# Maxima over partitions by TensorE and VectorE, and an order of work found in 40 passes, in a kernel of pooled attention and two MoE layers

## Chip, cores and metric

The kernel runs on one core of a Trainium2 chip. The metric is the time of one execution on the device in microseconds (us); less is better. The profile is that of one execution, taken by the hardware profiler.

## What is computed

Attention over 4 batches and 8 heads of 64, whose 1152 queries are averaged in pairs to 576, and then two feed-forward layers on the 2304 resulting rows of 512:

```python
q_pool = q.reshape(B, H, S // 2, 2, D).mean(axis=3)
scores = np.matmul(q_pool, k.transpose(0, 1, 3, 2)) / np.sqrt(D)
attn = np.exp(scores - np.max(scores, axis=-1, keepdims=True))
attn = attn / (np.sum(attn, axis=-1, keepdims=True) + 1e-09)
x = np.matmul(attn, v)                # then (B * 576, H * D)
h = x @ w_in                          # 512 -> 2048
x = (h / (1.0 + np.exp(-h))) @ w_out  # 2048 -> 512
a, b = x @ w1, x @ w2                 # 512 -> 1024 each
out = (a * b @ w3) @ w_out2           # 1024 -> 1024 -> 512
```

The weights come as float64; the outputs are float32.

## The kernel before

Matrix products with float32 operands take several passes on TensorE, so the kernel splits most operands into two float16 halves (`hi` and `lo`, scaled by a power of two) and adds three products (`TERMS`). The scale needs the largest absolute value of the tensor. VectorE reduces along the free dimension to one value per partition, and `allmax` (line 309) reduces over the 128 partitions on GpSimd, for the 12 stagings of V (line 431), the 9 blocks of attention output (line 653), the two first weights (line 768), w1 and w2 together (line 887) and the 6 inputs of the last stage: 30 in all. `pow2` (line 301) makes the power of two from it.

Attention goes by batch, half of the queries (`g`), pair of heads (`hp`), and tile of 128 queries, 144 tiles in all. `tile_ops` (line 446) issues one tile: scores into PSUM (`qk`, L465), the row maxima (L502, VectorE), the exponentials with their sum (L482, ScalarE), the inverse of the sum (L487, L490). In batches 1 to 3 the probabilities are split into halves (L530, L493) and transposed by a DMA (L498). In batch 0 (`b < WHOLE`) there are no halves: TensorE transposes the float32 tile (L514), ScalarE copies it out (L517), and the inverse of the sum is laid out by a VectorE tile `dg` (L523) and a small float32 matmul (`spread`, L562). Scores and transposes share two PSUM tiles of three banks (`t_s`). `pv_ops` (line 585) multiplies by V (L610, or L555 in batch 0) into one of two one-bank PSUM tiles (`t_mm`) and evacuates to `x32`, a float32 buffer for a block of 256 rows by 512; there is one such buffer, and one for the 64-row tails of the four batches.

`block_ops` (line 626) takes a block through the first MoE: the maximum of `x32` (L632), the all-reduce, the scales, the halves `x16` (L656, L643), eight `h_unit` steps (L676, two times twelve matmuls each), the gate on ScalarE and VectorE, its halves (L698 on ScalarE, L701 on GpSimd), and sixteen `x_unit` steps (L717). There are nine blocks, two per batch and one of the tails. `weights_moe1` (line 738) turns w_in and w_out, 16 chunks of 128 x 512 each, from float64 to float32 by integer operations (`from_f64`, L328 to L330), takes their maxima (L760) and splits them (L783, L788). After attention its buffers are given to the second MoE: w1, w2 and w_out2 are turned and split, w3 is multiplied by w_out2 beforehand (L1015), and six blocks of 384 rows run through L1119 and L1163.

The order of work on each engine is not the program's. Every step is an `op` with an engine, an estimated cost, a due time (`key`) and the buffers that it reads and writes; `Plan.run` (line 115) is a list scheduler that simulates the engines with these costs. At each turn it takes, of the steps that an engine could start within 0.15 us, the one with the smallest key:

```python
go = max(free[e], min(at for at, _ in can))
at, o = min(((at, o) for at, o in can if at <= go + 0.15), key=lambda x: (x[1].key, x[1].n))
```

The keys are written by hand, in units of attention tiles (for instance `i - 1.5` for the scores of tile `i`, `key - 12` for the halves of the gate). The instructions are then issued in the order that this one pass gives, and each engine works through its own list strictly in that order. All loads, stores and DMA transposes are issued from the queue of SP.

Of the kernel before, what the change touches and what calls it, by code (L numbers as in the profile page):

```python
# [9 lines left out]
F32 = mybir.dt.float32  # L10
# [17 lines left out]
LOAD_AFTER = 3.0  # L28
AFTER = {PE: 0.25, ACT: 0.2, DVE: 0.15, POOL: 0.2, SP: 0.0}
# [28 lines left out]
class Op:  # L58
    __slots__ = (
        "eng", "cost", "land", "fn", "key", "after", "need", "ready", "start", "end", "takes", "bufs", "n", "hook",  # L60
        "placed",
# [3 lines left out]
class Plan:  # L65
# [5 lines left out]
    def op(self, eng, cost, fn, r=(), w=(), key=0.0, land=None):  # L71
# [3 lines left out]
        o.n, o.hook = len(self.ops), None  # L75
# [39 lines left out]
    def run(self):  # L115
        cand = defaultdict(list)
        free = {e: 0.0 for e in ENGINES}
        free["CTL"] = 0.0
        order = []
# [17 lines left out]
        while any(cand.values()):  # L137
# [11 lines left out]
            assert best is not None, [o.n for some in cand.values() for o in some][:20]  # L149
            at, e, o = best  # L150
            cand[e].remove(o)
            o.start = at
            if e != "CTL":
                free[e] = at + o.cost
            o.end = at + (o.cost if o.land is None else o.land)
# [3 lines left out]
            for buf in o.takes:  # L159
                tag = buf.tag  # L160
                buf.place = min(tag.free, key=lambda s: (tag.free[s], s))
                del tag.free[buf.place]
                tag.next += 1
            for buf in o.bufs:
                buf.left -= 1
                buf.end = max(buf.end, o.end + AFTER.get(e, 0.0))
                if buf.left == 0:
                    buf.tag.free[buf.place] = buf.end
            for x in o.after:
# [15 lines left out]
def kernel(  # L185
# [51 lines left out]
    ident_b = Buf(Tag(1))  # L237

# [27 lines left out]
    t_dg = tags(attn, "dg", 4, [P, D])  # L266
# [42 lines left out]
    def allmax(dst, src):  # L309
        nc.gpsimd.partition_all_reduce(dst, src, channels=P, reduce_op=bass_isa.ReduceOp.max)  # L310

    def from_f64(dst, words, dst_b, words_b, key):
# [20 lines left out]
        op(DVE, 1.85, merge, [words_b], [dst_b], key + 0.01)  # L333
# [13 lines left out]

    kts, qts, v16s, mvs = {}, {}, {}, {}
# [14 lines left out]
    def prep_q(b, g, hp):  # L363
# [20 lines left out]
        op(DVE, 0.7 + 0.13 * g, pool, [qs], [qt], i0 - 7)  # L384

    def prep_v(b, hp):
        i0 = FIRST_T[(b, 0, hp)]
        v16, mv = attn_buf(t_v16), attn_buf(t_mv) if b >= WHOLE else None
# [10 lines left out]

        def top():  # L400
            nc.vector.reduce_max(mv.t[:, 0:1], vs.t, axis=AX.X, apply_absolute_value=True)

        def scales():
            pow2(mv.t[:, 1:2], mv.t[:, 2:3], mv.t[:, 3:4])
            nc.vector.tensor_scalar_mul(mv.t[:, 3:4], mv.t[:, 3:4], 2.0 ** 13)
            nc.vector.tensor_scalar_mul(mv.t[:, 4:5], mv.t[:, 2:3], 2.0 ** -29)

        def hi():
            d_, s_ = parts()
            nc.scalar.activation(d_[:, :, 0, :], s_, AF.Copy, scale=mv.t[:, 3:4])  # L410

        def lo():
            d_, s_ = parts()
            nc.vector.scalar_tensor_tensor(
                d_[:, :, 1, :], s_, mv.t[:, 3:4], d_[:, :, 0, :], op0=ALU.mult, op1=ALU.subtract
            )
# [13 lines left out]
        op(DVE, 1.36, top, [vs], [(mv, 0)], i0 - 4)  # L430
        op(POOL, 0.4, lambda: allmax(mv.t[:, 1:2], mv.t[:, 0:1]), [(mv, 0)], [(mv, 1)], i0 - 3.9)
        op(DVE, 0.8, scales, [(mv, 1)], [(mv, 2)], i0 - 2)
        op(ACT, 1.26, hi, [vs, (mv, 2)], [(v16, 0)], i0 - 1)
        op(DVE, 1.45, lo, [vs, (mv, 2), (v16, 0)], [(v16, 1)], i0 + 0.5)

    WHOLE = 1
    pts = {}
    x32s = {}  # L440
    dgs = {}

# [3 lines left out]
    def tile_ops(i):  # L446
# [53 lines left out]
        op(PE, 1.14, qk, [kt, qt], [sc], i - 1.5)  # L500
# [4 lines left out]
        op(ACT, 1.43, soft_exp, [sc, (sm, 0)], [e, (sm, 1)], i - 3.0 * whole)  # L505
        op(DVE, 0.32, inverse, [(sm, 1)], [(sm, 2)], i + 0.2)
        if whole:
            st, dg = Buf(t_s), attn_buf(t_dg)
            dgs[i] = dg
# [9 lines left out]
            op(PE, 1.1, turn32, [e, ident_b], [st, (pt, (j % 2, 0))], i + 0.3)  # L519
# [13 lines left out]
        op(DVE, 1.45, lo, [e, (sm, 2), (p16, 0)], [(p16, 1)], i + 0.8)  # L533
        op(SP, 2.75, turn, [p16], [(pt, j % 2)], i + 1, land=5.2)

    def pv_whole(b, g, hp, i, last, ps, nn, mine, x32, off):
# [22 lines left out]
        def spread():  # L559
            for (a, jj), dg in inv.items():  # L560
# [3 lines left out]
                    dg.t,  # L564
# [6 lines left out]
        op(  # L571
            PE, 0.3 if last else 0.6, spread, [ident_b] + [dg for k_, dg in inv.items() if not last or k_ == (0, 0)],
# [3 lines left out]
        op(PE, 1.4 if last else 4.5, pv, [v16] + list(mine.values()), [ps, (x32, (hp, off, 0))], i + 2.5)  # L576
# [8 lines left out]
    def pv_ops(b, g, hp, i, last=False):  # L585

        v16, mv = v16s[(b, hp)], mvs[(b, hp)]
# [4 lines left out]
        if blk not in x32s:  # L592
            x32s[blk] = attn_buf(t_x32t if last else t_x32)
        x32 = x32s[blk]
# [23 lines left out]

        def evac():
            nc.scalar.activation(x32.t[:, hp, off : off + nn], ps.t[:, :nn], AF.Copy, scale=mv.t[:, 4:5])  # L620

        op(PE, 1.2 if last else 2.95, pv, [v16] + list(mine.values()), [ps, (x32, (hp, off, 0))], i + 2.5)
        op(ACT, 0.3 if last else 0.45, evac, [ps, (mv, 2)], [(x32, (hp, off))], i - SOON)


    def block_ops(blk, i, span):

        x32, xm = x32s[blk], moe_buf(t_xm)
        x16 = moe_buf(t_x16)
# [612 lines left out]
```

## Time and profile before

| | |
|---|---|
| median of 3 runs | 1200.62 us (1199.74 to 1205.22) |
| the profiled execution | 1200.74 us |
| its span, first to last instruction | 1198.7 us |
[...]
| TensorE (PE) busy | 1108.2 us, 92% |
| VectorE (DVE) busy | 792.2 us, 66% |
| ScalarE (ACT) busy | 663.2 us, 55% |
| GpSimd (POOL) busy | 158.1 us, 13% |

The shares are means over stages that differ: batch 0's attention with the weights of the first MoE (to about 250 us), attention of batches 1 to 3 beside the first MoE (to 755 us), the last blocks of the first MoE beside the weights of the second (to 860 us), and the second MoE. PE is TensorE's matmuls, PEld its weight loads, which run beside them. An idle time is put down to what ended it; "issue" means that nothing that the profile shows ended it.

### The profile page before, as it was taken

What the parts mean: (1) busy time and instruction counts of PE and PEld (TensorE: products, weight loads), DVE (VectorE), ACT (ScalarE), POOL (GpSimd) and SP (SyncE); (2) the same over time, 40 slices, a digit from 0 to 9 for tenths busy, and PEclk for the clock granted to TensorE, in tenths of its full rate; (3) what the DMA queues carried; (4) which work ended last, traced back from release to release, by engine and by line L of the source; (5) the groups of instructions that cost most, each with busy time, mean ns of one, the idle gap of its engine ahead of it and who ended that gap; (6) DMA issues with size and microseconds to landing.
All of it is one profiled execution on the core that took longest, in us unless ns stands there. A gap on an engine that the chain in (4) does not pass through costs nothing.

```text
span 1198.7 us, 21922 instructions
## 1 busy us (share of the span) xinstructions
PE 1108.2 (92%) x8972; PEld 809.1 (67%) x8972; DVE 792.2 (66%) x1283; ACT 663.2 (55%) x986; POOL 158.1 (13%) x156
## 2 busy tenths in 40 slices
PE   3778897999999999999899999897999999999998
PEld 2445675767776767677677777786756776767666
DVE  6988898498788788797987785576977521212110
ACT  3656667567677577686686675465634322222221
POOL 0000120012012012020020020112121111111211
PEclk9978998999999999999999999898999999999999
DMA  9635344368988997989979778454334001010001
GB/s 348 211 134 184 115 140 157 115 136 169 181 182 171 218 194 166 190 174 200 199 145 200 151 123 148 147 194 137 124 123 150 1 27 54 12 42 27 10 18 27
DMA packets 294821, 163.17 MB, mean 136 GB/s; under 512 B 256064, under 2 KB 266816, under 8 KB 294720
## 3 DMA queue, kind: packets, MB, share of 16 engines
q1 hardware_dynamic: 294720, 161.77, 55.6%
q8 instruction: 70, 1.15, 0.4%
q14 instruction: 31, 0.25, 0.1%
HBM read 80.22 MB, written 9.44 MB: 75 GB/s over the span
## 4 chain that ended last, share of the span: by engine, by line
PE 51%; DVE 3%; issue 2%; DMA 1%; ACT 1%; POOL 1%; DVEq 0%; POOLq 0%; ACTq 0%
PE mt L1119 10%; PE mm L676 7%; PE mt L1163 6%; PE mm L717 5%; PE sc L465 5%; PE mm L1119 4%; PE mm L610 4%; PE mt L1015 3%; PE mt L676 3%; PE mt L717 2%; PE mm L1163 2%; DMA pt<-p 1%; PE mm L1015 0%; DVE sm L502 0%; DVE x L643 0%
## 5 line engine op out<-in xcount | busy, mean ns | idle before, releaser
L465 PE MATMUL sc<-kt,qt 64*128 64x128 f32 (+3 forms) x960 | 200.7, 534 | 29.0 <-ACT pt L517 20.9
L502 DVE TENSOR_REDUCE sm<-sc 128x1 f32<-128x1152 f32 x144 | 193.9, 1348 | 40.5 <-PE sc L465 40.2
L676 PEld LDWEIGHTS <-w 128*128 128x128 f16 x1728 | 169.7, 100 | 60.6 <-issue 35.9
L482 ACT ACTIVATE e<-sc,sm 128x1152 f32<-128x1152 f32 x144 | 175.2, 1217 | 47.9 <-DVE sm L502 42.8
L717 PEld LDWEIGHTS <-w 128*128 128x128 f16 x1728 | 164.3, 98 | 54.2 <-issue 30.9
L676 PE MATMUL mm<-x,w 128*128 128x256 f16 x1440 | 173.2, 279 | 18.6 <-DVE x L643 9.7
L493 DVE SCALAR_TENSOR_TENSOR p<-e,sm,p 128x1152 f16<-128x1152 f32 x108 | 159.5, 1484 | 29.7 <-ACT p L530 29.2
L717 PE MATMUL mm<-g,w 128*128 128x256 f16 x1440 | 169.8, 273 | 2.8 <-POOL g L701 1.9
L465 PEld LDWEIGHTS sc<-kt,qt 64*128 64x128 f32 (+1 forms) x960 | 91.8, 182 | 97.9 <-issue 57.1
L530 ACT ACTIVATE p<-e,sm 128x1152 f16<-128x1152 f32 x108 | 134.2, 1248 | 31.4 <-DMA pt<-p 10.7
L701 POOL TENSOR_TENSOR g<-t,g 128x512 f16<-128x512 f32 x72 | 94.6, 1319 | 297.8 <-ACT g L698 237.0
L1139 DVE SCALAR_TENSOR_TENSOR abf<-mt,x2m,asb 128x384 f32<-128x384 f32 x36 | 22.1, 615 | 123.9 <-PE mt L1119 123.9
L610 PE MATMUL mm<-pt,v 128*64 128x256 f16 (+1 forms) x1944 | 89.8, 250 | 5.3 <-DMA pt<-p 5.1
L610 PEld LDWEIGHTS <-v 128*64 128x64 f16 x1944 | 81.9, 112 | 13.4 <-DMA pt<-p 6.6
L1119 PEld LDWEIGHTS <-w1h 128*128 128x128 f16 x576 | 56.1, 99 | 41.5 <-issue 6.2
L1119 PEld LDWEIGHTS <-w2h 128*128 128x128 f16 x576 | 56.2, 98 | 38.0 <-issue 1.3
L1119 PE MATMUL mt<-x2h,w2h 128*128 128x384 f16 x432 | 76.1, 326 | 0.0
L1119 PE MATMUL mt<-x2h,w1h 128*128 128x384 f16 x384 | 69.4, 331 | 2.1 <-DVE x2h L1081 1.5
L514 PE MATMUL sc<-identr,e 128*128 128x128 f32 x324 | 50.1, 308 | 17.9 <-ACT e L482 17.8
L692 ACT ACTIVATE t<-mm,xm 128x512 f32<-128x512 f32 x60 | 41.1, 685 | 38.4 <-PE mm L676 35.0
L514 PEld LDWEIGHTS sc<-identr,e 128*128 128x128 f32 x324 | 41.1, 158 | 30.1 <-ACT e L482 25.2
L517 ACT COPY pt<-sc 128x1152 f32<-128x1152 f32 x36 | 40.3, 1118 | 32.1 <-PE sc L514 31.9
(131 smaller groups left out, 1336.1 us busy)
## 6 DMA issues: line engine op xcount, KB each, us to landing
v<-in_moe_w_dram SPq DMA_DIRECT2D x32, 512.0 KB, 4.2
qs<-in_q_dram SPq DMA_DIRECT2D x16, 640.0 KB, 4.8
kt<-in_k_dram SPq DMA_DIRECT2D x16, 576.0 KB, 4.6
qs<-in_q_dram SPq DMA_DIRECT2D x16, 512.0 KB, 4.5
g<-in_moe_w_in_dram SPq DMA_DIRECT2D x16, 512.0 KB, 6.1
w<-t SPq DMA_DIRECT2D x32, 256.0 KB, 3.3
stage<-in_v_dram SPq DMA_DIRECT2D x12, 576.0 KB, 4.6
x2d<-t SPq DMA_DIRECT2D x36, 128.0 KB, 2.3
```

The lines of the kernel that those rows point to most:

```text
L465: nc.tensor.matmul(sc.t[cols, bank, : (c1 - c0) * P], qt.t[rows * D : (rows + 1) * D, 4 if last else 2 * h + j - 2 * g, cols], kt.t[rows * ...
L482: nc.scalar.activation(e.t, flat(), AF.Exp, bias=sm.t[:, 0:1], accum_out=sm.t[:, 1:2])
L493: nc.vector.scalar_tensor_tensor(p16.t[:, 1], e.t, sm.t[:, 3:4], p16.t[:, 0], op0=ALU.mult, op1=ALU.subtract)
L502: DVE, 1.36, lambda: nc.vector.tensor_reduce(sm.t[:, 0:1], flat(), axis=AX.X, op=ALU.max, negate=True),
L514: nc.tensor.transpose(to[:, c * P : (c + 1) * P], e.t[:, c * P : (c + 1) * P], ident)
L530: ACT, 1.27, lambda: nc.scalar.activation(p16.t[:, 0], e.t, AF.Copy, scale=sm.t[:, 3:4]),
L610: nc.tensor.matmul(ps.t[a * D : (a + 1) * D, :nn], v16.t[:, a, KEYS[c], tv, :], rhs, start=idx == 0, stop=idx == 3 * NK - 1,)
L676: nc.tensor.matmul(ps.t[:, f % 2 * BL : (f % 2 + 1) * BL], w16[0][ct * NQ + f // 4][:, tw, (f % 4) * P : (f % 4 + 1) * P], x16.t[:, ct, tx ...
L701: nc.gpsimd.tensor_tensor(gv(1), two(g32), gv(0), op=ALU.subtract)
L717: nc.tensor.matmul(ps.t[:, :BL], w16[1][f][:, tw, ct * P : (ct + 1) * P], gs[u].t[:, f % 4, tg, :], start=f == 0 and n == 0, stop=f == NF ...
L1119: nc.tensor.matmul(ps.t[:, :TB], buf.t[:, ct, tw, f * P : (f + 1) * P], xr.t[:, ct, tx, :], start=idx == 0, stop=idx == 11,)
L1163: nc.tensor.matmul(ps.t, ab[f].t[:, ta, m * P : (m + 1) * P], w3_b.t[:, f, tb, :], start=f == 0 and n == 0, stop=f == NF2 - 1 and n == 2,)
```

## The change

It does five things.

1. `Plan.run` calls the list scheduler (now `go`) 40 times. After a pass that is the best so far by the modelled end, `late` computes for each step the latest start that would not move that end, back along the dependencies and along the buffers that one step frees for another. The next pass's keys are the best pass's keys, moved by a random share towards these latest starts, plus random noise. The order of the best pass is issued. The first pass has the hand-set keys.
2. A step on TensorE has a `mode`; a change of mode costs 0.1 us in the model. Many cost estimates are changed by a few per cent.
3. `top_mm` takes the place of `allmax`: a float32 matmul of the column, broadcast to 128 columns, with the identity puts the 128 values into every partition's row of a PSUM tile (one of `t_mm`), and VectorE reduces along the row. There are 24 of them.
4. In batches 1 to 3 the scale of the attention output is no longer taken from the output but from the maxima of V, which bound it. The blocks with `g == 1`, and the last pair of heads of those with `g == 0`, no longer go through `x32`: ScalarE and VectorE write their halves from PSUM. The tail block's bound is put together from the V maxima and, for batch 0, a reduction over its columns.
5. The tile `dg` goes: `spread` reads the inverse as a broadcast column. Each tile's scores are linked behind those of the tile before and, in batch 0, behind the transposes of the tile three before.

```diff
     def run(self):
+        some = random.Random(1)
+        best, keys = None, None
+        for n in range(ROUNDS):
...
+            order = self.go()
+            if order is not None:
+                end = max(o.end for o in order)
+                if best is None or end < best[0]:
+                    best = end, [(o, o.start, o.end) for o in order], [(b, b.place) for b in bufs]
+                    keys = [o.key for o in self.ops], self.late(order, end)
+            part, noise = some.random(), 6.0 * some.random() ** 2
+            for o, key, last in zip(self.ops, keys[0], keys[1]):
+                o.key = key + part * (last - key) + noise * some.gauss(0.0, 1.0)
...
+    def late(self, order, end):
+
+        first = {}
+        for o in sorted(order, key=lambda o: (-o.start, -o.n)):
+            last = end
+            gap = AFTER.get(o.eng, 0.0)
+            for x in o.after:
+                last = min(last, first[x] - (0.0 if x.eng == o.eng and o.land is None else gap))
+            for x in o.frees:
+                last = min(last, first[x] - gap - (LOAD_AFTER if x.eng == SP else 0.0))
+            first[o] = min([last - o.end + o.start] + [first[x] for x in o.placed])
+        return [first[o] for o in self.ops]
...
+            if e == PE and o.mode != mode:
+                late, mode = SWITCH, o.mode
...
-    t_sm = tags(attn, "sm", 8, [P, 4])
-    t_mv = tags(attn, "mv", 6, [P, 5])
+    t_sm = tags(attn, "sm", 12, [P, 4])
+    t_mv = tags(attn, "mv", 2, [P, 6, NP])
...
-    def allmax(dst, src):
-        nc.gpsimd.partition_all_reduce(dst, src, channels=P, reduce_op=bass_isa.ReduceOp.max)
+    def top_mm(dst, src, r, w, key):
+
+        am = Buf(t_mm)
+        op(
+            PE, 0.3,
+            lambda: nc.tensor.matmul(am.t[:, :P], src().to_broadcast([P, P]), ident, start=True, stop=True),
+            [r], [am], key,
+        )
+        op(DVE, 0.22, lambda: nc.vector.reduce_max(dst(), am.t[:, :P], axis=AX.X), [am], [w], key)
...
+        if hp == NP - 1:
+            xm = xms[2 * b]
+            op(
+                DVE, 0.15, lambda: nc.vector.reduce_max(vmx[:, b : b + 1], mv.t[:, 1, :], axis=AX.X),
+                [(mv, (h_, 1)) for h_ in range(NP)], [(vmx_b, b)], i0 - 1.9,
+            )
+            op(DVE, 0.8, lambda: x_scales(xm, vmx[:, b : b + 1]), [(vmx_b, b), wst_b[0]], [(xm, 2)], i0 - 1.9)
...
-        op(PE, 1.14, qk, [kt, qt], [sc], i - 1.5)
+        scores = op(PE, 1.19, qk, [kt, qt], [sc], i - 1.5, mode=1)
+        if i - 3 in turns:
+            plan.link(scores, {turns[i - 3]})
+        if i:
+            plan.link(scores, {asked[i - 1]})
+        asked[i] = scores
...
-            op(
-                DVE, 0.2,
-                lambda: nc.vector.tensor_scalar(
-                    dg.t, ident[:, :D], 0.0, sm.t[:, 3:4], op0=ALU.mult, op1=ALU.add
-                ),
-                [(sm, 2), ident_b], [dg], i + 0.6,
-            )
...
-                    dg.t,
+                    dg.t[:, 3:4].to_broadcast([P, D]),
...
+        straight = b >= WHOLE and not last and (g == 1 or hp == NP - 1)
...
+            op(PE, 2.95, pv, [v16] + list(mine.values()), [ps], i + 2.5, mode=2)
+            op(ACT, 0.4, x_hi, [ps, (mv, 9)], [(x16, (hp, 0))], i - SOON)
+            op(DVE, 0.42, x_lo, [ps, (mv, 9), (x16, (hp, 0))], [(x16, (hp, 1))], i - SOON)
+            return
...
-        op(POOL, 0.4, lambda: allmax(xm.t[:, 1:2], xm.t[:, 0:1]), [(xm, 0)], [(xm, 1)], i - 6)
...
+        elif not bound:
+            op(DVE, 1.25, top, [x32], [(xm, 0)], i - 6)
+            top_mm(lambda: xm.t[:, 1:2], lambda: xm.t[:, 0:1], (xm, 0), (xm, 1), i - 6)
```

## Rows read from the trace of the kernel before

**Rows 1.** The page: busy time (share of the span); granted clock in 40 slices.
```profile
PE 1108.2 (92%) x8972; PEld 809.1 (67%) x8972; DVE 792.2 (66%) x1283; ACT 663.2 (55%) x986; POOL 158.1 (13%) x156
...
PEclk9978998999999999999999999898999999999999
```
**Rows 2.** Busy time by stage: stretch, length, PE, PEld, DVE, ACT, POOL, clock, DMA.
```profile
20.00:124.00 104.00, 75.22 (x441) 47.90 (x442) 93.67 (x187) 64.51 (x92) 1.14 (x3) 0.89 0.54 187
124.00:250.00 126.00, 116.44 (x1003) 83.30 (x1003) 99.40 (x193) 79.93 (x116) 12.51 (x14) 0.95 0.41 132
250.00:755.00 505.00, 485.00 (x4954) 366.64 (x4950) 405.33 (x596) 355.23 (x487) 70.98 (x60) 0.99 0.89 175
755.00:860.00 105.00, 90.71 (x811) 78.75 (x804) 78.15 (x126) 63.53 (x121) 21.27 (x20) 0.95 0.44 145
860.00:1199.00 339.00, 331.54 (x1761) 227.52 (x1758) 106.36 (x171) 93.78 (x162) 51.54 (x53) 0.99 0.15 49
```
**Rows 3.** Waits of TensorE, whole span: total us, times, longest.
```profile
PE sc L465 <- ACT pt L517: 20.9, 17, 2.0
PE sc L514 <- ACT e L482: 17.8, 8, 7.0
PE mm L676 <- DVE x L643: 9.7, 8, 1.9
PE mt L717 <- POOL g L701: 9.6, 2, 8.9
PE mm L676 <- ACT x L656: 8.2, 6, 3.5
```
**Rows 4.** Timeline of TensorE: start, duration, instructions [idle before, releaser].
```profile
60.11 1.83 PE L514 MATMUL sc<-identr,e 128*128 128x128 f32 x9 [2.07 <-ACT e L482]
63.15 2.50 PE L465 MATMUL sc<-kt,qt 64*128 64x128 f32 x6 [1.21 <-ACT pt L517]
...
70.90 1.20 PE L514 MATMUL sc<-identr,e 128*128 128x128 f32 x9
72.03 1.35 PE L465 MATMUL sc<-kt,qt 64*128 64x512 f32 x6
...
123.82 0.27 PE L676 MATMUL mm<-x,w 128*128 128x256 f16 x1
```
**Rows 5.** Groups of TensorE, first 124 us: busy us, mean ns, idle before.
```profile
L465 PE MATMUL sc<-kt,qt 64*128 64x128 f32 (+1 forms) x120 | 36.0, 671 | 24.1 <-ACT pt L517 16.7 <-DVE qt L379 6.9 <-ACT e L482 0.6
L514 PE MATMUL sc<-identr,e 128*128 128x128 f32 x171 | 29.0, 328 | 15.3 <-ACT e L482 15.3
```
**Rows 6.** Groups of VectorE, first 124 us; the last line over the whole span.
```profile
L760 DVE TENSOR_REDUCE wmx<-w 128x1 f32<-128x512 f32 x21 | 14.3, 680 | 0.3
...
L328 DVE TENSOR_SCALAR w<-w 128x512 int32<-128x512 int32 x22 | 9.2, 418 | 0.0
...
L329 DVE SCALAR_TENSOR_TENSOR w<-w,w 128x512 int32<-128x512 int32 x3 | 2.1, 692 | 0.1
...
L523 DVE TENSOR_SCALAR dg<-identr,sm 128x64 f32<-128x64 f32 x36 | 8.7, 249 | 5.7 <-PE mm L562 5.5
```
**Rows 7.** Group of VectorE, whole span: the maximum of a block.
```profile
L632 DVE TENSOR_REDUCE xm<-x 128x1 f32<-128x1024 f32 x8 | 9.7, 1215 | 8.9 <-ACT x L620 8.7
```
**Rows 8.** GpSimd: two lines of its timeline, and its waits for L701.
```profile
826.18 0.38 POOL L310 PARTITION_ALL_REDUCE ws<-ws  x1 [6.15 <-issue]
834.59 3.38 POOL L701 TENSOR_TENSOR g<-t,g 128x512 f16<-128x512 f32 x3 [8.04 <-issue]
...
POOL g L701 <- issue: 46.0, 8, 8.0
```
**Rows 9.** Group of TensorE, whole span: the spread of batch 0.
```profile
L562 PE MATMUL mm<-identr,dg 128*64 128x128 f32 (+1 forms) x80 | 8.0, 321 | 0.0
```
**Rows 10.** The chain that ended last: start, us, what.
```profile
514.45 2.73 PE mm L676 x24
...
527.40 5.35 PE mm L676 x48
```

More of the change, by code (lines that the diff above doesn't have):

```diff
@@ L5 @@
 import concourse.tile as tile
-from concourse import bass_isa, mybir
+from concourse import mybir
 from concourse._compat import with_exitstack
@@ L115, in run, with go @@
     def run(self):
+        bufs = {id(b): b for o in self.ops for b in o.bufs}.values()
+        tags = {id(b.tag): b.tag for b in bufs}.values()
+        ops = [(o, o.need, o.ready) for o in self.ops]
+        left = [(b, b.left) for b in bufs]
+        free = [(t, dict(t.free)) for t in tags]
+        some = random.Random(1)
+        best, keys = None, None
+        for n in range(ROUNDS):
+            for o, need, ready in ops:
+                o.need, o.ready, o.frees = need, ready, []
+            for b, n_ in left:
+                b.left, b.end, b.place, b.users = n_, 0.0, None, []
+            for t, f in free:
+                t.free, t.next, t.last = dict(f), 0, {}
+            order = self.go()
[7 more added lines that the diff above has]
+                o.key = key + part * (last - key) + noise * some.gauss(0.0, 1.0)
+        for b, place in best[2]:
+            b.place = place
+        for o, start, stop in best[1]:
+            o.start, o.end = start, stop
+        return [o for o, _, _ in best[1]]
+    def late(self, order, end):
[9 more added lines that the diff above has]
+        return [first[o] for o in self.ops]
+    def go(self):
         cand = defaultdict(list)
@@ L148, in run @@
                     best = at, e, o
-            assert best is not None, [o.n for some in cand.values() for o in some][:20]
+            if best is None:
+                return None
             at, e, o = best
@@ L152, in run @@
             o.start = at
+            late = 0.0
+            if e == PE and o.mode != mode:
+                late, mode = SWITCH, o.mode
             if e != "CTL":
-                free[e] = at + o.cost
-            o.end = at + (o.cost if o.land is None else o.land)
+                free[e] = at + o.cost + late
+            o.end = at + (o.cost if o.land is None else o.land) + late
             order.append(o)
@@ L162, in run @@
                 del tag.free[buf.place]
+                for x in tag.last.get(buf.place, ()):
+                    x.frees.append(o)
                 tag.next += 1
@@ L168, in run @@
                     buf.tag.free[buf.place] = buf.end
+                    buf.tag.last[buf.place] = buf.users
             for x in o.after:
@@ L237 @@
     ident_b = Buf(Tag(1))
+    vmx = const.tile([P, B + 1], F32, name="vmx")
+    vmx_b = Buf(Tag(1))
     def tags(pool, name, n, shape, dt=F32, fifo=True):
@@ L570, in pv_whole @@
         sp, rs = Buf(t_mm), attn_buf(t_rs)
-        op(
-            PE, 0.3 if last else 0.6, spread, [ident_b] + [dg for k_, dg in inv.items() if not last or k_ == (0, 0)],
+        first = op(
+            PE, 0.3 if last else 0.6, spread, [ident_b] + [(dg, 2) for k_, dg in inv.items() if not last or k_ == (0, 0)],
             [sp, (rs, 0)], i + 1.0,
@@ L662, in block_ops @@
+        if not (bound and g):
+            got = [(x32, (h_, 0)) for h_ in range(n_)] if bound else [x32]
+            to = [[(x16, (h_, t)) for h_ in range(n_)] for t in range(2)]
+            op(ACT, 0.15 + 0.25 * n_, hi, got + [(xm, 2)], to[0], i - 6)
+            op(DVE, 0.15 + 0.27 * n_, lo, got + [(xm, 2)] + to[0], to[1], i - 6)
         units = NF // 2 + 4 * NC
@@ L723, in x_unit @@
                             )
-                op(PE, 1.3, x_unit, [gs[u]] + [w16_b[1][f] for f in range(4 * u, 4 * u + 4)], [ps], key)
+                op(PE, 1.33, x_unit, [gs[u]] + [w16_b[1][f] for f in range(4 * u, 4 * u + 4)], [ps], key)
                 key += step
@@ L819 @@
                     pv_ops(b, g, hp, i0 + 4, last=True)
+            if g and b < WHOLE:
+                x32t = x32s[2 * B]
+                cols = slice(b * TAIL, (b + 1) * TAIL)
+                op(
+                    DVE, 0.4,
+                    lambda x32t=x32t, cols=cols: nc.vector.reduce_max(
+                        vmx[:, B : B + 1], x32t.t[:, :, cols], axis=AX.XY, apply_absolute_value=True
+                    ),
+                    [(x32t, (h_, b * TAIL)) for h_ in range(NP)], [(vmx_b, B)], i0 + 9,
+                )
+                top_mm(
+                    lambda b=b: vmx[:, b : b + 1], lambda: vmx[:, B : B + 1], (vmx_b, B), (vmx_b, b), i0 + 9
+                )
             ready[2 * b + g] = i0 + 4 + g + 3.5
```

152 lines of the change are left out of this document (92 added, 60 removed).

## The prediction

> **What bounds the kernel now.** I read the page first, then the busy times by stage, then TensorE's waits, and only then single stretches. TensorE is busy for 1108 of 1198.7 us [rows 1], so 90 us is all that any order of the same work could take out of its idle time. [...] The view by stage says where the 90 us lie [rows 2]. From 20 to 124 us TensorE idles 29 us and VectorE is 90% busy; before 20 us lie 11 more, mostly the first loads (the five stages hold 1098.9 of the 1108.2 us busy, so 9.3 of the first 20). From 250 to 755 us, the long overlap of attention and the first MoE, TensorE is at 96% and loses 20 us in 505. The change of stage at 755 to 860 us loses 14, the second MoE after it 7. So this is a TensorE-bound kernel with a VectorE-bound start, and a gain can only be: a shorter start, the stalls at the seams, or less TensorE work.
>
> The waits of TensorE name the stalls [rows 3]: 20.9 and 17.8 us are batch 0's (a score tile waits for its PSUM bank, a transpose waits for the exponentials), 9.7 + 8.2 us are first matmuls of a MoE block that wait for the two halves of their input, and 9.6 us, 8.9 of it at once, is a wait for GpSimd.
>
> What a gap costs beyond itself is seen at 60 us [rows 4]: after 2.07 us of idling the nine transposes take 1.83 us and the next scores 2.50, where at 70.90 and 72.03 they take 1.20 and 1.35. These two groups alone lose 1.8 us. Over the first 124 us the 120 score matmuls (six to a tile, 20 tiles) take 36.0 us, 1.80 a tile against 1.35, and the 19 groups of transposes 29.0 us, 1.53 against 1.20 [rows 4, 5]: 9 + 6 = 15 us of lower clock.
>
> **The change, part by part.**
>
> *The start.* The first MoE block begins at 123.8 us [rows 4]. It needs w_in and 16 tiles of batch 0, but by then VectorE has also turned six chunks of w_out (L328 ran 22 times, and w_in has 16 chunks), which no matmul reads before the block's second half: each is 0.42 + 2 x 0.69 (L329, and L330 is its like) + 0.68 = 2.48 us [rows 6], six are 15 us. A priority taken from the chain to the end ranks them behind what the block waits for; the hand-set one gives them a due time. The dg tiles (36 of 0.25 us, half of them before 124 us) go too. I take **-15 us**. Bounds: nothing, if the 27 us that VectorE has free between 124 and 250 us [rows 2] don't hold the chunks, because then x_unit waits for w_out, which is late next; and -38 us, all that the waits for L517 and L482 add up to [rows 3]. The 15 is nearest to a row of work that can really move, so it stands.
>
> *The seams between MoE blocks.* For batches 1 to 3 the bound of attention's output is taken from the maxima of V, which are known early; the chain evacuate, reduce (L632, 1.21 us [rows 7]), all-reduce, scale, two halves, shrinks to two operations per pair of heads. The waits of L676 are 17.9 us [rows 3]; blocks 0 and 1 keep their reduction and the tail block keeps its two halves, about 6 us by my share of them. **-12 us**, between 0 and -17.9. What is late next: a PV result now holds its PSUM buffer (two in all) until both halves are read from it.
>
> *GpSimd's all-reduces.* All 30 go. At 826.18 us one of them runs 0.38 us, and GpSimd's next product starts only at 834.59 us after 8.04 us in which nothing that the profile shows held it [rows 8]; TensorE waits 8.9 us for that product. Over the run GpSimd sits 46.0 us in eight such gaps before L701 [rows 8]. With the all-reduces gone the gaps go, except the first. Of the 9.6 us of waits [rows 3] I take all, and 1.4 for smaller ones behind them: **-11 us**, bounds 0 (if the w1/w2 scales are late next, since they now wait for a matmul in TensorE's queue) and -14, the whole idle time of that stage.
>
> *The clock.* From 755 to 860 us the granted clock is 0.95, 5 us of full-speed time, and from 250 to 755 us 0.99, another 5 [rows 2]. Half of it should go with the gaps: **-5 us**, between 0 and -10; the start's 15 us I leave, since VectorE will still starve it.
>
> *The new maxima.* 24 of them (12 for V, 2 + 1 for weights, 6 for the last stage's input, blocks 0 and 1, batch 0's tail) cost a matmul of 128 columns in fp32 and a VectorE reduction of 128 elements from PSUM, which no row shows. Lower bound of the matmul: 0.13 us, a ninth of a group of transposes [rows 4]; nearest row: the spread L562, a lone fp32 matmul of the same width, 0.32 us [rows 9]. 24 x 0.32 = 7.7 us. Each also breaks a run: a lone h_unit takes 2.73 us, two in a row 5.35 [rows 10], so breaking a run costs 2 x 2.73 - 5.35 = 0.11 us, 2.6 us for 24. Together **+10 us**, between +3 and +15. [...]
>
> *VectorE.* It gains the 24 reductions, between 0.25 us (L523, 64 wide) and 0.68 (L760, 512 wide) each [rows 6], about 7 us, and 15 halves straight from PSUM in place of larger ones; it loses the 36 dg tiles (8.7 us) and seven reductions of 1.21 [rows 6, 7]. Net -9 us or so, which I cost at nothing: after 250 us it is hidden by TensorE, busy 485 of 505 us. If that cover went, it would be a gain.
>
> *The second MoE* keeps its operations; with 331.5 of 339 us busy, some 3 of the rest being the final store, the order there is worth nothing. *Store and load queues*: no DMA is added; SP only gets another order.
>
> Sum: -15 - 12 - 11 - 5 + 10 = -33 us. The profiled execution took 1200.74 us (2.0 beyond its span), the median of the runs is 1200.62: the same. **1200.7 - 33 = 1168 us.**
>
> **The rivals.**
> 1. *The chip doesn't follow the planner's order.* The 40 passes pick the best of their own model, whose costs know neither the lower clock nor transfers that collide; hand-set keys may have been as good. Then the start and the clock give nothing: -12 - 11 + 10, 1188 us. For it: the start's loss is half clock, which the model doesn't know. Against: VectorE's early w_out work is plain in the rows. Chance 0.18, spread 1176 to 1202.
> 2. *TensorE stalls at the maxima (the slower side).* Today a late reduction holds up GpSimd, which idles anyway; now the matmul stands in TensorE's in-order queue and whatever follows it (scores, h_unit) waits with it for VectorE's reduction. A gap like the one at 60 us costs 2.07 + 1.8 = 3.9 us. It decides from nine of the 24 on (33 / 3.9); at the twelve of V, each behind a 1.3 us reduction in the stage where TensorE has 4% to spare, 47 us: 1215 us. Against: L676's waits on VectorE average only 9.7 / 8 = 1.2 us. Chance 0.17.
> 3. *The start fills further.* If two thirds of the 38 us go and a third of the 15 us of clock with them, it is -31 instead of -15: 1152 us, and 1136 with all of it. Against: VectorE is at 90% there. Chance 0.10.
> 4. [...] If entering and leaving each new matmul waits out a lone one, 48 x 0.32 = 15 us instead of 2.6: 1180 us. [...] Chance 0.07.
>
> **How the numbers follow.** The forecast, 0.48, has its own range of 1150 to 1186: two of the three gains at their ends. The range of 8 in 10 takes in rivals 1, 3 and 4 to their ends, and leaves out rival 2, under 0.2: **1135 to 1204 us**. 0.5%, 6 us, is about what a measurement of this kernel can tell from no change. Faster by more: the forecast 0.48, rival 3 0.10, rival 4 0.07 and 0.10 of rival 1, 0.75. Within 0.5%: 0.06 of rival 1 and 0.01 of rival 2, 0.07. Slower: 0.16 of rival 2 and 0.02 of rival 1, 0.18.
>
> **What would show it.** In the profile after: the first L676-like matmul starts near 105 us rather than 124 (start); first matmuls of blocks 2 to 7 no longer wait for input halves (seams); no 8 us gap of GpSimd and no TensorE wait of several us near the change of stage; TensorE's busy time minus lower clock up by about 10 us, with a line of 24 matmuls. Wrong would be: waits of TensorE on the maxima's reductions of more than some 10 us in all (rival 2), an idle time before 250 us as large as now (rival 1), or a mean of the new matmuls' slots near 0.6 us (rival 4).

## The result and the profile after

The changed kernel took **1144.59 us** (median of 4 runs, 1143.56 to 1146.19) where the kernel before, on the same chip, took 1202.19 (1199.74 to 1205.22): a ratio of 0.9521, 95% interval 0.9493 to 0.9549. The forecast was 1168, so the direction was right, the range held, and the gain was 57 us where 33 was forecast. The profiled execution took 1143.56 us, 1.8 beyond its span of 1141.8; the mean granted clock was 0.983.

The page of the kernel after, busy time and granted clock in 40 slices (against [rows 1]):

```profile
PE 1092.6 (96%) x9020; PEld 810.9 (71%) x9020; DVE 785.4 (69%) x1266; ACT 655.6 (57%) x983; POOL 149.6 (13%) x126
...
PEclk9978999999999999999999999998999999999999
```

TensorE idles 1141.8 - 1092.6 = 49.2 us instead of 90.5, and its busy time fell by 15.6 although 48 matmuls (two for each of 24 maxima) were added. Idle time -41.3, busy time -15.6: together the -56.9 us of the span.

Where the idle time went is read from three stretches: the start, the overlap of attention and the first MoE, and the rest (the kernel after is further on at each border). First the kernel before, by stage (stretch, length, PE, PEld, DVE, ACT, POOL, clock, DMA, GB/s):

```profile
0.00:250.00 250.00, 200.98 (x1470) 136.17 (x1472) 202.39 (x393) 150.65 (x216) 14.34 (x23) 0.92 0.50 172
250.00:700.00 450.00, 432.02 (x4324) 324.39 (x4320) 370.64 (x551) 322.29 (x441) 65.26 (x56) 0.99 0.90 179
700.00:1200.00 500.00, 475.24 (x3189) 348.51 (x3186) 219.20 (x341) 190.24 (x330) 78.53 (x77) 0.98 0.29 79
```

And the kernel after, the same columns, with the stretch before its first MoE matmul as a last line:

```profile
0.00:250.00 250.00, 213.50 (x1674) 151.45 (x1675) 217.35 (x406) 167.29 (x241) 13.15 (x16) 0.94 0.57 186
250.00:700.00 450.00, 449.16 (x4630) 343.80 (x4629) 380.91 (x572) 329.27 (x457) 62.88 (x46) 1.00 0.94 185
700.00:1200.00 500.00, 429.98 (x2721) 315.69 (x2718) 187.14 (x290) 159.09 (x285) 73.57 (x64) 0.99 0.21 67
20.00:112.00 92.00, 68.60 (x427) 45.37 (x424) 88.22 (x167) 60.63 (x90) 0.00 (x0) 0.86 0.59 205
```

Length (to the end of the span in the last stretch) less PE gives the idle time: 49.0 to 36.5 us at the start, 18.0 to 0.8 in the overlap, 23.5 to 11.8 after it.

TensorE's waits after, whole span (total us, times, longest; against [rows 3]):

```profile
PE sc L615 <- ACT e L578: 11.8, 8, 3.9
PE mm L370 <- DVE sm L583: 7.7, 2, 6.7
...
PE mt L370 <- DVE x2m L1215: 6.2, 1, 6.2
PE sc L561 <- ACT pt L618: 6.1, 7, 1.7
PE mm L832 <- POOL g L816: 0.5, 1, 0.5
PE mm L791 <- DVE vmx L373: 0.4, 1, 0.4
PE mm L791 <- DVE x L723: 0.2, 1, 0.2
```

L561, L615, L791 and L832 are the old L465, L514, L676 and L717; L370 and L373 are the new matmul and its reduction. The seams, where the first matmul of a block waits for its input, went from 17.9 us to 0.6, GpSimd's products from 9.6 to 0.5, batch 0's two waits from 38.7 to 17.9. New are 13.9 us at L370, nearly all of it at two maxima. The timeline of TensorE shows these two and the first matmuls of the first block's halves (start, duration, instructions, [idle before, releaser]):

```profile
82.70 0.80 PE L370 MATMUL mm<-identr,wst 128*128 128x128 f32 x2 [6.70 <-DVE sm L583]
...
111.81 3.66 PE L791 MATMUL mm<-x,w 128*128 128x256 f16 x24
...
172.06 1.47 PE L832 MATMUL mm<-g,w 128*128 128x256 f16 x12
...
788.28 0.77 PE L370 MATMUL mt<-identr,x2m 128*128 128x128 f32 x2 [6.23 <-DVE x2m L1215]
```

The block starts at 111.81 us instead of 123.82 [rows 4]; its second half at 172.06 instead of 202.97.

The first stall stands behind the last reductions of w_in itself, the second behind two slow passes of a weight conversion. One group of VectorE up to 82.5 us, then VectorE's and GpSimd's timeline of the kernel after, the lines around both:

```profile
L391 DVE TENSOR_SCALAR w<-w 128x512 int32<-128x512 int32 x22 | 9.2, 416 | 0.5 <-ACT w L387 0.5
...
76.65 5.42 DVE L875 TENSOR_REDUCE wmx<-w 128x1 f32<-128x512 f32 x9
...
778.31 2.72 POOL L816 TENSOR_TENSOR g<-t,g 128x512 f16<-128x512 f32 x2 [2.57 <-ACT g L813]
...
778.46 1.56 DVE L392 SCALAR_TENSOR_TENSOR wfb<-v,wfb 128x512 int32<-128x512 int32 x1
780.05 1.53 DVE L393 SCALAR_TENSOR_TENSOR wfb<-v,wfb 128x512 int32<-128x512 int32 x1
...
781.95 0.69 DVE L392 SCALAR_TENSOR_TENSOR wfb<-v,wfb 128x512 int32<-128x512 int32 x1
...
786.40 1.74 DVE L1215 TENSOR_REDUCE x2m<-x2s 128x1 f32<-128x1536 f32 x1
```

At 76.65 VectorE is at nine L875 for 5.42 us. They are the last of w_in's 16, which its maximum needs: by 111.8 us L875 has run 16 times in all. By 82.5 us VectorE had converted 22 chunks (L391), w_in's 16 and, ahead of that maximum, six of w_out. At 778 the same pass takes 1.56 and 1.53 us beside GpSimd's products and 0.69 at 781.95; L1215, whose result TensorE waits for at 788.28, comes last.

### The profile page after: what moved, and what is told of

Read it like the earlier page. It is cut to its first block, busy times and chain, and to the rows that moved or that the text cites. A ratio compares the mean times of both kernels' runs of the same rounds, so it can differ in the third digit from the quotient of the medians.

```text
span 1141.8 us, 21857 instructions
## 1 busy us (share of the span) xinstructions
PE 1092.6 (96%) x9020; PEld 810.9 (71%) x9020; DVE 785.4 (69%) x1266; ACT 655.6 (57%) x983; POOL 149.6 (13%) x126
## 4 chain that ended last, share of the span: by engine, by line
PE 78%; DVE 13%; issue 3%; ACT 3%; DMA 3%; SPq 0%; DVEq 0%; ACTq 0%
PE mm L832 13%; PE sc L561 12%; PE mt L1247 12%; PE mm L791 11%; PE mm L708 7%; PE mt L1291 6%; PE mm L1247 4%; PE mt L1143 4%; PE mm L1291 3%; DVE w L392 2%; PE mm L649 2%; DVE sm L603 2%; PE sc L615 2%; DVE w L391 2%; DVE wmx L875 1%
## 5 line engine op out<-in xcount | busy, mean ns | idle before, releaser
L561 PE MATMUL sc<-kt,qt 64*128 64x128 f32 (+3 forms) x960 | 192.8, 522 | 15.5 <-DVE qt L443 6.9
L832 PEld LDWEIGHTS <-w 128*128 128x128 f16 x1728 | 166.5, 98 | 36.3 <-issue 14.9
L791 PEld LDWEIGHTS <-w 128*128 128x128 f16 x1728 | 166.7, 98 | 32.2 <-issue 11.0
L816 POOL TENSOR_TENSOR g<-t,g 128x512 f16<-128x512 f32 x72 | 96.2, 1344 | 688.4 <-ACT g L813 529.6
L832 PE MATMUL mm<-g,w 128*128 128x256 f16 x1488 | 173.6, 274 | 0.5 <-POOL g L816 0.5
L791 PE MATMUL mm<-x,w 128*128 128x256 f16 x1440 | 166.1, 274 | 0.7 <-DVE vmx L373 0.4
L561 PEld LDWEIGHTS sc<-kt,qt 64*128 64x128 f32 (+1 forms) x960 | 91.9, 179 | 82.0 <-issue 56.8
L708 PE MATMUL mm<-pt,v 128*64 128x256 f16 (+1 forms) x1944 | 88.2, 248 | 0.8 <-DMA pt<-p 0.4
L708 PEld LDWEIGHTS <-v 128*64 128x64 f16 x1944 | 80.5, 111 | 9.4 <-issue 6.3
L1247 PE MATMUL mt<-x2h,w2h 128*128 128x384 f16 x456 | 78.7, 326 | 0.0
L1247 PE MATMUL mt<-x2h,w1h 128*128 128x384 f16 x396 | 68.2, 326 | 0.0
L615 PE MATMUL sc<-identr,e 128*128 128x128 f32 x324 | 47.6, 300 | 11.8 <-ACT e L578 11.8
L615 PEld LDWEIGHTS sc<-identr,e 128*128 128x128 f32 x324 | 40.0, 154 | 22.5 <-ACT e L578 18.1
L1278 POOL TENSOR_TENSOR abr<-abf,abr 128x384 fp32r<-128x384 f32 x28 | 31.5, 1136 | 184.9 <-ACT abr L1273 184.9
L618 ACT COPY pt<-sc 128x1152 f32<-128x1152 f32 x36 | 39.8, 1119 | 27.2 <-PE sc L615 27.1
```

What stands on the lines that cost most here:

```text
L561: nc.tensor.matmul(sc.t[cols, bank, : (c1 - c0) * P], qt.t[rows * D : (rows + 1) * D, 4 if last else 2 * h + j - 2 * g, cols], kt.t[rows * ...
L615: nc.tensor.transpose(to[:, c * P : (c + 1) * P], e.t[:, c * P : (c + 1) * P], ident)
L708: nc.tensor.matmul(ps.t[a * D : (a + 1) * D, :nn], v16.t[:, a, KEYS[c], tv, :], rhs, start=idx == 0, stop=idx == 3 * NK - 1,)
L791: nc.tensor.matmul(ps.t[:, f % 2 * BL : (f % 2 + 1) * BL], w16[0][ct * NQ + f // 4][:, tw, (f % 4) * P : (f % 4 + 1) * P], x16.t[:, ct, tx ...
L816: nc.gpsimd.tensor_tensor(gv(1), two(g32), gv(0), op=ALU.subtract)
L832: nc.tensor.matmul(ps.t[:, :BL], w16[1][f][:, tw, ct * P : (ct + 1) * P], gs[u].t[:, f % 4, tg, :], start=f == 0 and n == 0, stop=f == NF ...
```

## The experiments

All ratios are to the kernel before on the same chip, with 95% intervals. Unless a text says otherwise the edit is to the changed kernel. The theory: two gains, one of the new work (maxima, bound) and one of the order, which add. The rivals: the order does nothing on the chip, or the work does nothing without it.

### The new work in the order by hand: one pass

```diff
-ROUNDS = 40
+ROUNDS = 1
```

> The changed kernel with ROUNDS = 1: the new work in the order of the hand-set keys. Theory A (the order found in 40 passes gives most of the 57 us): 1180 to 1200 us, and TensorE's waits at the seams and in the start come back, idle time 75 us or more. Theory B (the changed work gives most: no GpSimd maxima, bounds known early, no dg): within 15 us of the changed kernel, 1145 to 1160 us.

Measured 0.9686 (0.9651 to 0.9721), 1166.15 us, between the two ranges that were expected. The new work alone, with its links and changed cost estimates, is worth 3.1%. By stage, and one of TensorE's waits:

```profile
0.00:250.00 250.00, 201.41 (x1504) 138.68 (x1504) 199.44 (x367) 151.73 (x219) 10.66 (x14) 0.95 0.51 172
250.00:700.00 450.00, 442.79 (x4494) 335.18 (x4492) 376.95 (x581) 329.07 (x453) 64.57 (x47) 1.00 0.95 183
700.00:1200.00 500.00, 459.11 (x3027) 337.41 (x3024) 205.04 (x319) 179.16 (x313) 72.88 (x65) 0.99 0.26 76
```
```profile
PE sc L615 <- ACT e L578: 16.5, 5, 9.5
```

The seams' waits for input halves are gone (0.2 us are left), the start's are not: the first L791 came at 133.15 us, later than before.

### The old work in the new order

The planner's new functions in the kernel before, whose operations are kept; it has no forms to switch between, so that cost is 0.

```diff
+ROUNDS = 40
+SWITCH = 0.0
...
+                o.key = key + part * (last - key) + noise * some.gauss(0.0, 1.0)
```

> The kernel before with the new Plan.run alone (40 passes, no mode cost; its own costs, GpSimd maxima, dg, and x32 for every block). Theory A: 1155 to 1175 us, since the order is what counts. Theory B: 1190 to 1205 us, since the order can't shorten the chain of reduction, all-reduce and halves, and the 8 us gaps of GpSimd stay.

Measured 0.9795 (0.9768 to 0.9822), 1179.69 us, again between the two ranges. Its stages, and two of its waits (L772 and L731 are the old L717 and L676):

```profile
0.00:250.00 250.00, 198.93 (x1559) 139.42 (x1560) 213.00 (x420) 160.68 (x231) 14.85 (x24) 0.92 0.54 179
250.00:700.00 450.00, 428.70 (x4332) 324.47 (x4329) 363.21 (x532) 316.79 (x438) 69.61 (x57) 0.98 0.88 177
700.00:1200.00 500.00, 463.48 (x3085) 337.31 (x3084) 211.70 (x333) 184.39 (x319) 77.21 (x76) 0.99 0.27 78
```
```profile
PE mm L772 <- POOL g L756: 10.9, 2, 7.4
...
PE mm L731 <- ACT x L711: 5.2, 3, 3.4
```

3.1 + 2.0 = 5.2% against 4.8% for both: in the total the two add. Stage by stage they don't. TensorE's idle time, length less PE with the spans 1169.3 and 1177.6, in us (the profiled execution of the work alone, 1171.09, is the slowest of its four):

| | before | work alone | order alone | both |
|---|---|---|---|---|
| idle, 0 to 250 | 49.0 | 48.6 | 51.1 | 36.5 |
| idle, 250 to 700 | 18.0 | 7.2 | 21.3 | 0.8 |
| idle, after 700 | 23.5 | 10.2 | 14.1 | 11.8 |
| busy | 1108.2 | 1103.3 | 1091.1 | 1092.6 |
| mean granted clock | 0.974 | 0.987 | 0.972 | 0.983 |
| matmuls by 250 us | 1470 | 1504 | 1559 | 1674 |

The work alone takes 24 us out of the overlap and the end. The order alone takes 4 us of idling in all, but 17 us of busy time. The start's idle time falls by 12.5 us only with both, but by 250 us the order alone too has done more matmuls than the kernel before, with as much idling.

The busy time is shorter although the mean granted clock looks unchanged (0.972 against 0.974). That mean misleads. In each trace the record of the clock begins with a first rise, and a view counts what lies ahead of it as full clock. It begins at 39.8 us in the kernel before, at 42.7 with one pass, and at 11.0 with the old work in the new order and in the changed kernel. TensorE's timeline, nine transposes in the kernel before and then with the old work in the new order:

```profile
26.13 2.18 PE L514 MATMUL sc<-identr,e 128*128 128x128 f32 x9 [7.00 <-ACT e L482]
...
22.24 1.20 PE L569 MATMUL sc<-identr,e 128*128 128x128 f32 x9
```

The view gives two levels where the clock stands still: in the kernel before 0.50 of the full one from 63 to 66 us and 1.00 from 70 to 73. The 2.18 us are those of the lower level (2.18 again at 42.33 us in the second trace, where the recorded clock is at that level), the 1.20 those of the full one [rows 4]. So the kernel before ran its first 40 us at the lower level, in a stretch for which the view gives a clock of 1.00, its third number from the end. That line, and the sums over this stretch and all the recorded ones at the lower level, for the kernel before, the old work in the new order and the changed kernel:

```profile
0.00:39.81 39.81, 19.80 (x63) 11.81 (x64) 27.81 (x52) 15.92 (x22) 0.69 (x6) 1.00 0.84 301
...
sum 101.27, PE 68.23 PEld 43.44 DVE 69.76 ACT 48.77 POOL 4.51; mean PE 5.69 PEld 3.62 DVE 5.81 ACT 4.06 POOL 0.38
...
sum 75.83, PE 39.75 PEld 27.89 DVE 46.56 ACT 32.39 POOL 5.12; mean PE 3.98 PEld 2.79 DVE 4.66 ACT 3.24 POOL 0.51
...
sum 48.52, PE 33.29 PEld 23.43 DVE 38.48 ACT 27.27 POOL 0.85; mean PE 4.76 PEld 3.35 DVE 5.50 ACT 3.90 POOL 0.12
```

Six scores take 2.50 us at the lower level and 1.35 at the full one [rows 4], nine transposes 2.18 and 1.20, so about 0.46 of the time spent there is lost. As an estimate from these rows, 0.46 x (68.2 - 39.8) = 13 of the 17 us are the clock's; some 4 us stay open. In the order by hand TensorE stands 7.00 us before the transposes at 26.13. In all four profiles of that order (the kernel before, one pass, and two more below) the 64x512 scores of the first 40 us take 1.01 to 1.11 us in the mean, in the ten of a searched order 0.71 to 0.94. That the order brings the full level earlier is read from these traces; no run changes the clock alone.

### The maxima on GpSimd, in both orders

The 24 maxima as all-reduces on GpSimd again, the rest as changed; once with 40 passes, once with one.

```diff
-            PE, 0.3,
-            lambda: nc.tensor.matmul(am.t[:, :P], src().to_broadcast([P, P]), ident, start=True, stop=True),
-            [r], [am], key,
+            POOL, 0.4,
+            lambda: nc.gpsimd.partition_all_reduce(dst(), src(), channels=P, reduce_op=bass_isa.ReduceOp.max),
+            [r], [w], key,
...
-        op(DVE, 0.22, lambda: nc.vector.reduce_max(dst(), am.t[:, :P], axis=AX.X), [am], [w], key)
```

> The changed kernel with the maxima over partitions on GpSimd again (24 all-reduces instead of 24 matmuls and reductions), planned in 40 passes. If the all-reduces cost what the gaps of GpSimd cost before (46.0 us of gaps, 9.6 us of TensorE's waits), it is 5 to 15 us slower than the changed kernel, 1150 to 1160. If their place was harmless, it is faster: TensorE is rid of 11 us of matmuls and of waits of 13.9 us at L370, 1125 to 1140.

Measured with 40 passes 0.9546 (0.9518 to 0.9575), 1150.43 us. Waits of GpSimd and TensorE:

```profile
POOL x2m L369 <- issue: 30.8, 5, 6.9
...
POOL g L814 <- issue: 22.5, 3, 8.1
...
PE mm L830 <- POOL g L814: 5.0, 4, 3.2
```

> The changed work with GpSimd's all-reduces and a single pass: against e1_one_pass it isolates the maxima in the hand-set order, against the kernel before the rest of the work (bound, dg, links, costs). If the maxima are most of e1's gain of 38 us: 1185 us or more, with GpSimd gaps ahead of L814. If the rest is: 1165 to 1175 us.

Measured with one pass 0.9900 (0.9847 to 0.9952), 1188.57 us, and the same waits:

```profile
POOL g L814 <- issue: 51.9, 7, 8.2
...
PE mm L830 <- POOL g L814: 11.0, 4, 6.4
PE mt L830 <- POOL g L814: 5.6, 3, 3.7
```

Against 0.9686 the move of the maxima off GpSimd is worth 2.1% in the order by hand. Against 0.9521 it is worth 0.25% in the searched order, with intervals that overlap: the search keeps the all-reduces off the products that are due (22.5 us of gaps before L814 instead of 51.9) and TensorE's 24 maxima are saved (busy 1084.7 against 1092.6 us, 7.9). The gaps before the all-reduces of the last stage stay, 30.8 us (24.6 with one pass).

### The maxima alone, in the kernel before

The other half of that question: only the maxima moved, all 30 of them, no bound, no search.

```diff
-        op(POOL, 0.4, lambda: allmax(mv.t[:, 1:2], mv.t[:, 0:1]), [(mv, 0)], [(mv, 1)], i0 - 3.9)
+        top_mm(lambda: mv.t[:, 1:2], lambda: mv.t[:, 0:1], (mv, 0), (mv, 1), i0 - 3.9)
...
```

> The kernel before with top_mm in the place of allmax and nothing else: one pass, hand-set keys, 30 maxima by TensorE and VectorE. If the maxima's move is worth its 22 us (e6 against e1) by itself: 1172 to 1185 us. If it needs the early bound and the links to be worth that: 1190 to 1205 us, with TensorE waiting at the new matmuls for VectorE's reductions of x32.

Measured 1.0041 (1.0015 to 1.0067), 1209.01 us: no gain. In the profiled execution (1203.61, the fastest of twelve) the waits for GpSimd did go, but others came:

```profile
PE sc L472 <- ACT e L489: 19.1, 16, 2.9
...
PE mt L724 <- POOL g L708: 1.1, 2, 0.7
```

TensorE's waits for L708 are 1.1 us, and at the new matmuls it waits only 2.2 and 1.6 us, not long as was expected; but its score tiles now wait 19.1 us for the exponentials, in 16 pieces, where [rows 3] has no such wait of a score tile among its largest. So the 2.1% above belong to the maxima together with the rest of the changed work (bound, links, costs, no dg), not to the maxima by themselves. Which of those it needs was not tried, and each edit also gives another order, which no run holds fixed.

### Without the bound

Every block reduces its own maximum.

```diff
-        straight = b >= WHOLE and not last and (g == 1 or hp == NP - 1)
+        straight = False
...
-        bound = WHOLE <= b < B
+        bound = False
```

> The changed kernel without the bound from V: every block goes through x32, its own maximum and its halves, as before; maxima still by TensorE and VectorE, 40 passes. If the bound is what ended the waits of 18 us at the seams: 12 us slower or more, 1156 to 1165, with L791 waiting for the halves. If the order hides that chain anyway: within 5 us of 1144.6.

Measured 0.9588 (0.9559 to 0.9617), 1154.72 us, between what was expected of the two cases: beside the search it is 0.7%, 8 us, slower than with the bound. TensorE's waits for the input halves stay small all the same:

```profile
PE mm L791 <- ACT x L752: 1.6, 1, 1.6
PE mm L791 <- DVE x L755: 1.0, 1, 1.0
```

2.6 us, and 1.6 more at the matmuls of the blocks' maxima, not 17.9: with the search the long chain at a seam is hidden too. The 8 us are less than the 0.9% between two seeds of the search (next section), so they are not shown to be the bound's.

### The search's own parts

Without the random term, so that a key only moves towards the chain to the end; and, apart from that, with another seed.

```diff
-            part, noise = some.random(), 6.0 * some.random() ** 2
+            part, noise = some.random(), 0.0 * some.random() ** 2
```
```diff
-        some = random.Random(1)
+        some = random.Random(2)
```

> The changed kernel with the noise term set to zero: keys only move towards the latest starts. If the move along the chains to the end is what finds the order, as fast as the changed kernel or a little faster, 1132 to 1147 us. If the random noise is what finds it, near the single pass, 1155 to 1166 us.

> The changed kernel with another random seed. How far the result is luck of the draw: if the search is robust, 1138 to 1152 us; if the shown seed was a lucky one, 1155 us or more.

Measured without the random term 0.9502 (0.9457 to 0.9548), 1141.82 us; with seed 2 0.9609 (0.9566 to 0.9652), 1154.48, somewhat slower than the 1152 that was expected at most. The move along the chains is enough; with the random term the two seeds differ by 0.9%, and neither was better than none. So with one seed to each edit, a difference of less than some 0.9% between searched orders is not shown to be the edit's.

### The conversions of w_out held back

The step of the prediction done by force: each conversion of w_out linked behind the first block's halves.

```diff
-        op(ACT, 0.68, rebias, [words_b], [dst_b], key)
+        first = op(ACT, 0.68, rebias, [words_b], [dst_b], key)
...
+            if blk == 0:
+                for o in held[1]:
+                    plan.link(o, {halves})
```

> The changed kernel with all of w_out's conversions linked behind the input halves of the first MoE block, which is what the prediction thought the search would do. If that is how the start is shortened: the first L791 before 100 us, and no slower than 1144.6 us. If w_out is late next: the first L832 waits for w_out past 180 us, TensorE idles between 120 and 190 us, and the time is 1150 to 1165 us.

Measured 0.9510 (0.9462 to 0.9557), 1141.10 us: no different. TensorE's timeline, the first matmul of the first block's two halves (L795 and L836 are L791 and L832):

```profile
96.25 3.16 PE L795 MATMUL mm<-x,w 128*128 128x256 f16 x24
...
194.62 1.48 PE L836 MATMUL mm<-g,w 128*128 128x256 f16 x12
```

The block starts 15.6 us earlier than at 111.81 and its second half 22.6 us later than at 172.06. TensorE's wait at w_in's maximum falls from 6.7 to 0.7 us, yet it idles 36.7 us before 250 us, as in the changed kernel (36.5): the 6 us come back as smaller waits, 2.7 of them for batch 0's exponentials and copies, 2.1 for w_out's halves at L836.

### The stall at the second MoE's input

No random term, and the conversions of the second MoE's job planned at 2.4 us instead of 1.95, nearer to the slow passes at 778 us. Beside it, the held conversions without the random term, and the changed kernel again.

```diff
-    def from_f64(dst, words, dst_b, words_b, key):
+    def from_f64(dst, words, dst_b, words_b, key, cost=1.95):
...
-        op(DVE, 1.95, merge, [words_b], [dst_b], key + 0.01)
+        op(DVE, cost, merge, [words_b], [dst_b], key + 0.01)
...
-        from_f64(lambda: wf.t, lambda: w64.t, wf, w64, key)
+        from_f64(lambda: wf.t, lambda: w64.t, wf, w64, key, 2.4)
```

> e5 (no noise) with the conversion of float64 words in the second MoE's weights planned at 2.4 us instead of 1.95, since beside GpSimd its passes took 1.5 us instead of 0.69. If that misestimate is what held TensorE 6.2 us (3.5 us in e5) at the first x2m maximum: the wait goes below 1 us and the time is 1134 to 1140 us. If not, the time stays at e5's 1138 to 1145 us.

> e8 (w_out's conversions held behind the first block's input) and e5 (no noise) together. If both help, and in different places: 1130 to 1138 us. If each is only another draw of the search: 1138 to 1150 us.

> The changed kernel once more, on the same chip as e10 and e11, so that differences of a few us can be told: ratio 0.952 to the kernel before.

Measured 0.9451 (0.9419 to 0.9483), 1135.92 us; 0.9460 (0.9428 to 0.9491), 1138.61; and 0.9518 (0.9487 to 0.9549), 1145.10. The first is faster than both kernels. The second, at the border of its two ranges, shows no gain beyond either of its parts. Its maximum of the second MoE's input, on TensorE's timeline:

```profile
785.53 0.39 PE L370 MATMUL mm<-identr,x2m 128*128 128x128 f32 x2
```

No idle time stands before it; the 6.23 us are gone. The same kernel without the dearer conversion (0.9502) still waited 3.5 us there. The stall at w_in's maximum stays, 8.3 us in this kernel. That the dearer conversion by itself is faster than none is not shown: 0.9451 and 0.9502 have intervals that overlap.

## Why the prediction was right, and where it was wrong

**The start, -15.** TensorE idles 12.5 us less before 250 us. That this is near the forecast is luck, for **the step failed**: "A priority taken from the chain to the end ranks them behind what the block waits for" is not what happened. VectorE's groups in the kernel after, up to its first L791 at 111.8 us:

```profile
L391 DVE TENSOR_SCALAR w<-w 128x512 int32<-128x512 int32 x26 | 10.8, 417 | 0.5 <-ACT w L387 0.5
...
L875 DVE TENSOR_REDUCE wmx<-w 128x1 f32<-128x512 f32 x16 | 9.7, 675 | 0.0
...
L903 DVE SCALAR_TENSOR_TENSOR t<-w,wst,t 128x512 f16<-128x512 f32 x11 | 7.7, 744 | 0.0
```

26 chunks less w_in's 16 are ten chunks of w_out, where the kernel before had six. What was put off were the reductions for w_out's maxima (L875 16 times, L760 21 times [rows 6]) and the second splits (L903 11 times by then), and the dg tiles are gone; VectorE was busy 88.2 of the 92 us from 20 to 112, 96% against 90% [rows 2]. The larger gain is at the second half, 31 us earlier: w_out was ready for it, and where it was held back the half came 22.6 us later. That run shows that the predicted deferral is worth nothing. w_out is late next, as the lower bound had it, though TensorE hardly waits for it there (2.1 us); its idle time before 250 us is the same. With the old work the order alone leaves the idle time of the start at 51.1 us; what it gains there, 89 matmuls by 250 us, goes with the earlier rise of the clock, for which the start had no term.

**The seams, -12.** Mis-sized: L676's 17.9 us of waits went almost whole, the upper bound; the waits that I left to blocks 0, 1 and the tail are not there either. The run without the bound shows that the search hides those chains too, so the term belongs to bound and order together. With the old work, whose chain has GpSimd's all-reduce in it, the order alone leaves 9.2 us (5.2 for L711, 4.0 for L698).

**GpSimd's all-reduces, -11.** TensorE's waits went as forecast, 9.6 to 0.5 us, and so did the gaps: GpSimd's waits for L816 without a releaser are 7.7 us instead of 46.0 [rows 8]. As a price it was right for neither order: some 25 us in the order by hand (0.9900 against 0.9686), some 3 in the searched one, and nothing when the maxima were moved alone.

**The clock, -5.** The largest error of size. TensorE was busy at the lower level for 68.2 us before and 33.3 after, so with the 0.46 from above the clock gave some -16. About 7 of them lie after 250 us, where the forecast looked for at most 10. The other 9 lie in the start, and there the step failed: "the start's 15 us I leave, since VectorE will still starve it". VectorE is fuller than before (96%), and still the full level came at 11 us instead of 39.8. TensorE's busy time fell by 15.6 with 7.9 us of maxima in it, so the rest of its work took 23 us less: 16 by the clock, and some 7 that stay open and had no term in the sum.

**The new maxima, +10.** Right in size. Half of them are V's, and their reductions are the second line (groups of the kernel after, whole span):

```profile
L370 PE MATMUL mm<-identr,mv 128*128 128x128 f32 x24 | 5.5, 313 | 0.0
...
L373 DVE TENSOR_REDUCE mv<-mm 128x1 f32<-128x128 f32 x12 | 3.4, 284 | 1.5 <-PE mm L370 1.4
```

A maximum is two instructions of TensorE here, 5.5 / 12 = 0.46 us, where the forecast took the 0.32 of one and 0.11 for the break; all 24 together 11.3 us in the records, and 7.9 by the run that takes them away. A bare one was 0.39 us (at 785.53 us with the dearer conversion). So rival 4's 0.6 us didn't come. What the 0.46 is made of, no run shows.

**Rival 2, the stalls at the maxima.** It came true at two of 24 places, 13.9 us, above the "some 10 us" that I had set as its sign, yet the total is far from its 1215. V's twelve, on which the rival was priced, idle 0.0 us. The two that stall stand where VectorE is behind: in the filled start, and at the change of stage, where the planner's cost of a conversion was too low. The VectorE term, costed at nothing behind TensorE, was wrong there.

**Rival 1, the chip doesn't follow the planner.** Wrong for the total: the order was worth 2.0% on the old work and 1.7% on the new (0.8% with seed 2). But what it gives is not what the planner's chains were supposed to give. On the old work idle time hardly moved, and most of the gain is the clock's, which the planner's model doesn't know.

**Rival 3, the start fills further.** Its -31 for the start did not come: 12.5 us of idling and some 9 of clock are about -21. By its own terms "1136 with all of it" should read 1130: 38 + 15 in place of 15.

So -33 became -57 like this, in TensorE's time: idling in the start -12.5, and after 250 us -29 where the seams and GpSimd were to give -23; the clock -16 instead of -5; the maxima +8 instead of +10; and some -7 of other busy time that is not explained. The 13.9 us of new stalls are within the idle time.

## What to carry to other kernels

When a change reorders a schedule and changes the work, price the two against each other: a stall that is dear in one order can be hidden in the next (here the all-reduces cost 2.1% in the order by hand and 0.25% in the searched one), so a term taken from the waits of the old order holds for that order alone. On an engine that is nearly always busy, look at its busy time as well as its idle time, and at how long the same matmuls take in different stretches: an order in which TensorE was busy 39.8 us at the lower clock instead of 68.2 shortened the same work from 1108.2 to 1091.1 us, and the mean granted clock, 0.972 against 0.974, did not show it. Where a new instruction of the bound engine waits for another engine (6.70 and 6.23 us at two of the 24 places here), look for the few places where that other engine is full, rather than at the mean, and give the planner the cost which the pass has there.

## What the runs showed of the hardware

A VectorE pass with two int32 inputs took 1.56 and 1.53 us beside GpSimd's product of the same shape, and 0.69 us at 781.95, when that product had ended. Why it takes longer beside the product, no run shows.

GpSimd's gaps recur: in the run with all-reduces and one pass it stood 51.9 us in seven gaps before L814, up to 8.2 us each and 7.4 in the mean, and 46.0 us in eight, 5.8 in the mean, in the kernel before [rows 8]. What the engine does in a gap, no run shows.

Each float32 matmul of PV and of the maxima is two instructions of TensorE in the trace, each float16 one of PV is one. In the kernel before, 18 float32 matmuls of batch 0's PV took 4.11 us at 42.99, and the 54 float16 ones that do the same for a later batch 3.14 us at 306.94:

```profile
42.99 4.11 PE L555 MATMUL mm<-pt,v 128*64 128x256 f32 x36
...
306.94 3.14 PE L610 MATMUL mm<-pt,v 128*64 128x256 f16 x54
```
